# Windowed attention and FFN on one core: K and V blocks written from PSUM by two engines in place of DMA moves

## The chip, the cores and the metric

One Trainium2 chip, one core. The metric is the device time of one execution in microseconds (us), the median of the runs. Engines: PE is TensorE, DVE VectorE, ACT ScalarE, POOL GpSimd, SP SyncE (which here only issues DMAs).

## What is computed

Two layers of the same two blocks on x of 2048 rows by 512, in bf16: attention with 32 heads of 16 over a causal window of 256 keys, then a ReLU FFN of width 1792, each behind a layer norm and added to x.

```python
def _A_ref(x, wqkv, wo):
    H = 32; Dh = D // H; W = 256
    q, k, v = ...
    scores = jnp.einsum("bhqd,bhkd->bhqk", q, k) * (Dh ** -0.5)
    mask = (idx[:, None] - idx[None, :] >= 0) & (idx[:, None] - idx[None, :] < W)
    p = _softmax(jnp.where(mask[None, None], scores, -1e9), axis=-1)
    o = jnp.einsum("bhqk,bhkd->bhqd", p, v)
    return o.transpose(0, 2, 1, 3).reshape(B, S, D) @ wo
...
for layer in range(2):
    x = x + _A_ref(_layernorm(x), A_wqkv, A_wo)
    x = x + jnp.maximum(_layernorm(x) @ w1, 0) @ w2
```

## The kernel before

**Steps and slots.** The 2048 rows are cut into four chunks of 512 rows; two layers make eight steps, k = 0 to 7 (layer and chunk of a step are `divmod(k, 4)`). A step has twenty slots (`SPS`): four Q tiles t of 128 columns (eight heads of 16), and for each five groups g of key blocks (`GROUPS`, line 21). All 160 slots are written out in the loop at line 538. In a slot, in this order: the score matmuls of its group into the one score buffer `Sps` (`attn_group`, line 271, which ends with the exp on ScalarE into `Pb`); events planned for the slot; the first half of the slot's quota of projection and FFN matmuls (`run_tasks`); the masks of the group before (on VectorE, for groups 1 and 2 on GpSimd); the PV matmuls of the Q tile before, for one block of 128 rows (`pv_group`, into an accumulator `acc`, then VectorE's reciprocal and product into `O`); for the last Q tile of a step the DMA transpose of that row block of O into `OT` (`transpose_o`, line 344), whose output projection is planned two slots later; then the rest of the quota. So the PV matmuls of a step's last Q tile, its four OT transposes and its output projections O0 to O3 fall into slots 1 to 6 of the next step.

**Tasks.** A task is a group of 512-column matmuls into one PSUM bank of the pool `ps_d` (four banks, shared with `acc`) and its evacuation. The planner (`Task`, `run_tasks`, lines 403 to 432) takes among the tasks whose earliest slot has come the one with the earliest due time, and finishes it before it starts another. The quota of a slot is the number of matmuls left over the slots left, nine in most of the run and eight from step 6 on. `plan_qkv(k + 1)` plans the next chunk's K, Q and V for step k (lines 455 to 474). `plan_ffn` plans the FFN of a step when its fourth output projection is done; its w1 and w2 tasks run about one step later. `wo_done` (line 497) is called when an output projection's last matmul is issued: after O1 and after O3 it does half of the second norm (`ln_rows`: statistics on VectorE, power and products on GpSimd, then two DMA transposes into `xn2T` on SyncE's queue).

**Order.** Each engine's instructions go in the order in which the code issues them (`InOrder`, line 84), and SyncE's DMAs in one queue. An instruction that waits holds up all behind it on its engine.

**K.** K is needed as `KBD`: for each 64-key block two copies side by side, one with the odd heads' rows set to zero, one with the even heads' (e = 0, 1; the 16-row bands of a partition group). `KBD` is a ring of 20 blocks. In step 0 (`direct`) VectorE multiplies the PSUM bank by a 0/1 column of `par` per e, writing whole partitions. In the other steps ScalarE copies the bank to `Kst` (two buffers), and SyncE moves the bands, four per e, into `KBD`, whose other bands stay zero from the start (`k_items`, lines 220 to 246). Where a chunk's eight blocks wrap round the ring (the chunks made in steps 1 and 6) there are two runs of blocks, so 16 moves per tile and not 8.

**V.** `V2` holds per 64-key block two halves of 64 partitions, e = 0 and 1, 16 heads of 16 columns and a column of ones each. In step 0 VectorE copies four pieces of 64 partitions by 256 straight from PSUM; in the others it copies the bank to `Vst` (two buffers), and SyncE moves four pieces (`v_items`, lines 248 to 268).

**The chunk's norm.** `begin` (line 527) does the first norm of the next chunk in four slots from `SPS * k - 4`: statistics in slots 16 and 18 of the step before, application and the transposes into the one `xnT` buffer in slots 17 and 19. The Q tiles have five buffers.

Of the kernel before, what the change touches and what calls it, by code (L numbers as in the profile page):

```python
# [49 lines left out]
def kernel(  # L50
# [105 lines left out]
    KBD = const.tile([P, 4, NSLOT, 2, 64], BF16, name="KBD")  # L156
    V2f = const.tile([P, NSLOT * 544], BF16, name="V2f")
    V2 = V2f[:].rearrange("p (s e a d) -> p s e a d", s=NSLOT, e=2, a=16)
    Vst = [const.tile([P, 2, 16, 17], BF16, name=f"Vst{i}") for i in range(2)]
    for s0 in range(0, NSLOT, 4):  # L160
        nc.gpsimd.memset(V2f[:, 544 * s0:544 * (s0 + 4)].bitcast(FP32), 0.0)
        for e in range(2):
            nc.vector.memset(V2[64 * e:64 * e + 64, s0:s0 + 4, e, :, 16:17], 1.0)
    for t in range(4):
        nc.vector.memset(KBD[:, t, 8:NSLOT].rearrange("p a b c -> p (a b c)").bitcast(FP32), 0.0)
    for i in range(2):
        nc.vector.memset(Vst[i][:, :, :, 16:17], 1.0)
    PWALL = 20 * PW
    Pb = [const.tile([P, PWALL + 64], BF16, name=f"Pb{i}") for i in range(2)]
    for i in range(2):  # L170
# [38 lines left out]
    def q_items(xnT, Qt, t, direct=False):  # L209
        ps = []  # L210

        def one(kc):
            if kc == 0:
                ps.append(ps_d.tile([P, 512], FP32, name="ps_d"))
            mm(ps[0][:], wqkv[:, kc, t * P:(t + 1) * P], xnT[:, kc, :], kc == 0, kc == KC - 1)
            if kc == KC - 1:
                (act.copy if chained[0] and not direct else dve.tensor_copy)(Qt[:], ps[0][:])
        return [lambda kc=kc: one(kc) for kc in range(KC)]

    def k_items(layer, c, xnT, t, direct):  # L220
        ps = []
        s0 = slot(layer, 8 * c)
        runs = [(0, 8)] if s0 + 8 <= NSLOT else [(0, NSLOT - s0), (NSLOT - s0, 8)]

        def one(kc):
            if kc == 0:
                ps.append(ps_d.tile([P, 512], FP32, name="ps_d"))
            mm(ps[0][:], wqkv[:, kc, D + t * P:D + (t + 1) * P], xnT[:, kc, :], kc == 0, kc == KC - 1)
            if kc < KC - 1:
                return  # L230
            if not direct:
                Kst = work.tile([P, 512], BF16, name="Kst", bufs=2)
                act.copy(Kst[:], ps[0][:])
            for a, b in runs:
                sa = (s0 + a) % NSLOT
                for e in range(2):
                    if direct:
                        dve.tensor_scalar(out=KBD[:, t, sa:sa + b - a, e, :],
                                          in0=ps[0][:, 64 * a:64 * b].rearrange("p (s k) -> p s k", k=64),
                                          scalar1=par[:, e:e + 1], scalar2=None, op0=ALU.mult)  # L240
                        continue
                    for r in range(4):
                        rows = slice(32 * r + 16 * e, 32 * r + 16 * e + 16)
                        nc.sync.dma_start(KBD[rows, t, sa:sa + b - a, e, :],  # L244
                                          Kst[rows, 64 * a:64 * b].rearrange("p (s k) -> p s k", k=64))
        return [lambda kc=kc: one(kc) for kc in range(KC)]

    def v_items(layer, c, xnT, j, direct):
        ps = []

        def one(kc):
            if kc == 0:
                ps.append(ps_d.tile([P, 512], FP32, name="ps_d"))
            mm(ps[0][:], xnT[:, kc, j * P:(j + 1) * P], wqkv[:, kc, 2 * D:3 * D], kc == 0, kc == KC - 1)
            if kc < KC - 1:
                return
            v4 = ps[0][:].rearrange("p (a e d) -> p e a d", e=2, d=16)
            if not direct:
                dve.tensor_copy(Vst[j % 2][:, :, :, 0:16], v4)
            for half in range(2):  # L260
                sl = slot(layer, 8 * c + 2 * j + half)
                for e in range(2):
                    if direct:
                        dve.tensor_copy(V2[64 * e:64 * e + 64, sl, e, :, 0:16], v4[64 * half:64 * half + 64, e])
                    else:
                        nc.sync.dma_start(V2[64 * e:64 * e + 64, sl, e].rearrange("p a d -> p (a d)"),  # L266
                                          Vst[j % 2][64 * half:64 * half + 64, e].rearrange("p a d -> p (a d)"))
        return [lambda kc=kc: one(kc) for kc in range(KC)]


# [104 lines left out]
    def w2_items(c, hT, j, final):  # L375
        ps = []
        b = 4 * c + j

        def one(f):
            if f == 0:  # L380
                ps.append(ps_d.tile([P, 512], FP32, name="ps_d"))
            mm(ps[0][:], hT[:, f, j * P:(j + 1) * P], w2[:, f, :], f == 0, f == NF - 1)
            if f < NF - 1:
                return
            if final:
                ob = work.tile([P, D], BF16, name="ob", tag="Kst", bufs=2)
                dve.tensor_tensor(out=ob[:], in0=ps[0][:], in1=x_sb[:, b, :], op=ALU.add)
                nc.sync.dma_start(out_v[:, b, :], ob[:])
            else:
                dve.tensor_tensor(out=x_sb[:, b, :], in0=ps[0][:], in1=x_sb[:, b, :], op=ALU.add)  # L390
        return [lambda f=f: one(f) for f in range(NF)]
# [3 lines left out]
    SPS = 20  # L395
# [4 lines left out]
    def at_slot(s, fn):  # L400
        events.setdefault(s, []).append(fn)
# [53 lines left out]
    def plan_qkv(k, base):  # L455

        layer, c = divmod(k, NCH)

        def q_make(t):
            Q[k, t] = work.tile([P, 512], BF16, name="Qt", bufs=5)  # L460
            return q_items(xnTs[k], Q[k, t], t, k == 0)
        order = [("K0", 1), ("K1", 2.5), ("K2", 4), ("K3", 5.5), ("Q0", 7), ("V0", 8), ("V1", 9), ("V2", 10), ("V3", 11),
                 ("Q1", 12.5), ("Q2", 14.5), ("Q3", 17)]
        if k == 0:
            order = [("K0", 0), ("Q0", 0), ("V0", 1), ("V1", 1), ("V2", 1), ("V3", 1), ("K1", 2), ("Q1", 2), ("K2", 5),
                     ("Q2", 5), ("K3", 8), ("Q3", 8)]
        for what, due in order:
            n = int(what[1])
            if what[0] == "K":
                Task(base, base + due, base + SPS + 5 * n - 3, KC, lambda n=n: k_items(layer, c, xnTs[k], n, k == 0))  # L470
            elif what[0] == "Q":
                Task(base + 5 * n + 1 if k else 0, base + due, base + SPS + 5 * n - 1, KC, lambda n=n: q_make(n))
            else:
                Task(base + 7 if k else 0, base + due, base + SPS + 3, KC, lambda n=n: v_items(layer, c, xnTs[k], n, k == 0))

    def plan_ffn(k, s):
        layer, c = divmod(k, NCH)
# [48 lines left out]
    for k in range(NSTEP - 1):  # L526
        def begin(k=k, j=0, box={}):
            if j == 0:
                xnTs[k + 1] = work.tile([P, KC, 512], BF16, name="xnT", tag="xnT", bufs=1)
            if j % 2 == 0:  # L530
                box["s"] = ln_stats((k + 1) % NCH, "A", j, j + 2)
            else:
                ln_apply((k + 1) % NCH, xnTs[k + 1], "A", j - 1, j + 1, box["s"])
        for j in range(4):
            at_slot(max(2 + j // 2, SPS * k - 4 + j), lambda k=k, j=j, fn=begin: fn(k, j))
        plan_qkv(k + 1, SPS * k)
    masks = []
    for s in range(NS + 5):
# [88 lines left out]
    def run(items):  # L627
        for x in items:
            x()

    with tc.If(flag > 0):
# [64 lines left out]
```

## Time and profile before

| | us |
|---|---|
| median of 2 runs | 776.92 (776.37 to 777.47) |
| the profiled execution | 774.82 |
| its span, first to last instruction | 773.1 |
| PE busy | 527.7 (68%) |
| DVE busy | 330.2 (43%) |
| ACT busy | 317.1 (41%) |
| POOL busy | 254.2 (33%) |

The busy times are those of the profiled execution. Nearly all instructions have one line (94, the helper that records them), so groups are told apart by their tiles. SPq is SyncE's queue, whose instructions are DMA issues. PEclk is the granted TensorE clock as a share of 2.4 GHz; 0.50 is its lower level, 1.2 GHz. A window's row gives its limits and length, the busy us (and instructions) of PE, PEld, DVE, ACT and POOL, then PEclk, the DMA share and GB/s. A step's limits in time are the starts of its first exp and that of the next step's.

### The profile page before, as it was taken

How to read it: one execution, taken by the hardware profiler on the slowest of the kernel's cores; microseconds unless marked ns; L12 is line 12 of the kernel's file. 1: busy time of each engine (PE TensorE's matmuls, PEld its weight loads, DVE VectorE, ACT ScalarE, POOL GpSimd, SP SyncE). 2: the span in 40 equal slices, each digit the busy share in tenths (PEclk: the TensorE clock that was granted, in tenths of full speed). 3: DMA queues.
4: the chain of work that ended last, by engine and by line, in shares of the span. 5: the costliest groups of instructions: out<-in, count | busy, mean ns of one | idle time of the engine just before them, and what ended most of it. 6: DMA issues, size and time to landing. Idle time of an engine off the chain costs nothing.

```text
span 773.1 us, 14419 instructions
## 1 busy us (share of the span) xinstructions
PE 527.7 (68%) x5741; PEld 242.7 (31%) x5741; DVE 330.2 (43%) x869; ACT 317.1 (41%) x223; POOL 254.2 (33%) x558
## 2 busy tenths in 40 slices
PE   6656530459857797479857795579814689789576
PEld 2212310124323353134323342234301234434232
DVE  5822500237605472147515571257401455645541
ACT  2315722235544374345434353346513447736000
POOL 6432611042521345052523343053610342453100
PEclk8966565589968799778968898689966789979878
DMA  9312111121112211220212101220201210300200
GB/s 316 99 33 36 25 22 19 21 43 23 28 25 38 51 15 21 33 55 20 28 27 43 43 16 30 39 53 7 49 13 20 56 32 16 56 15 22 44 19 32
DMA packets 101244, 30.64 MB, mean 40 GB/s; under 512 B 85552, under 2 KB 100656, under 8 KB 101168
## 3 DMA queue, kind: packets, MB, share of 16 engines
q1 hardware_dynamic: 101168, 29.63, 17.9%
q8 instruction: 47, 0.77, 0.4%
q14 instruction: 29, 0.24, 0.1%
HBM read 7.86 MB, written 2.10 MB: 13 GB/s over the span
## 4 chain that ended last, share of the span: by engine, by line
PE 36%; SPq 22%; POOL 12%; DVE 11%; DMA 9%; issue 6%; ACT 3%; ACTq 0%; DVEq 0%; POOLq 0%
PE ps_d L94 28%; SPq L244 18%; PE acc L94 5%; POOL Pb L94 4%; PE Sps L94 4%; DMA OT<-O 4%; POOL xnA L94 3%; SPq L266 2%; DMA xnT<-xnA 2%; POOL xnB L94 2%; ACT Pb L94 2%; DVE stB L94 2%; DMA V2f<-Vst 2%; SPq L199 2%; DVE x_sb L94 1%
## 5 line engine op out<-in xcount | busy, mean ns | idle before, releaser
L94 ACT ACTIVATE Pb<-Sps 128x2048 bf16<-128x2048 f32 (+2 forms) x160 | 283.5, 1772 | 271.5 <-PE Sps L94 248.2
L94 POOL TENSOR_SCALAR_AFFINE_SELECT Pb<-Pb 64x256 bf16<-64x256 bf16 x368 | 154.4, 420 | 207.9 <-ACT Pb L94 182.9
L94 PE MATMUL ps_d<-xn2T,w 128*128 128x512 bf16 x448 | 128.7, 423 | 39.4 <-DMA xn2T<-xnB 25.4
L94 PE MATMUL ps_d<-wo,OT 128*128 128x512 bf16 x128 | 49.8, 541 | 102.6 <-DMA OT<-O 102.2
L94 PE MATMUL ps_d<-w,hT 128*128 128x512 bf16 x448 | 118.7, 395 | 0.8 <-DVE x_sb L94 0.8
L94 PEld LDWEIGHTS <-Pb 128*128 128x128 bf16 x2880 | 94.8, 99 | 46.7 <-issue 21.1
L94 PE MATMUL ps_d<-xnT,wqkv 128*128 128x512 bf16 x256 | 81.5, 445 | 37.4 <-DMA xnT<-xnA 33.1
L94 PE MATMUL acc<-V2f,Pb 128*128 128x34 bf16 x2880 | 96.3, 181 | 8.0 <-ACT Kst L94 4.5
L94 PE MATMUL Sps<-Qt,KBD 32*128 32x320 bf16 (+4 forms) x1408 | 67.6, 276 | 43.2 <-ACT Pb L94 42.1
L94 DVE TENSOR_TENSOR x_sb<-ps_d,x_sb 128x512 f32<-128x512 f32 x48 | 32.7, 689 | 148.1 <-PE ps_d L94 145.7
L94 DVE TENSOR_SCALAR hT<-ps_d 128x512 bf16<-128x512 f32 x112 | 76.8, 688 | 43.0 <-PE ps_d L94 42.6
L94 POOL TENSOR_TENSOR rstdB<-rstdB,mhalf 128x2 f32<-128x2 f32 x16 | 12.1, 759 | 200.8 <-DVE rstdB L94 200.8
L94 DVE RECIPROCAL chk<-acc 128x8 f32<-128x8 f32 x128 | 26.2, 204 | 117.7 <-PE acc L94 116.8
L94 PEld LDWEIGHTS <-w 128*128 128x128 bf16 x448 | 40.6, 104 | 93.6 <-issue 64.8
L94 DVE TENSOR_TENSOR Pb<-Pb,tri 128x512 bf16<-128x512 bf16 (+1 forms) x152 | 61.5, 436 | 16.1 <-ACT Pb L94 16.0
L94 PEld LDWEIGHTS <-KBD 32*128 32x128 bf16 x1408 | 24.7, 95 | 114.6 <-issue 112.0
L94 ACT CAST Kst<-ps_d 128x512 bf16<-128x512 f32 x28 | 16.0, 587 | 98.3 <-DMA KBD<-Kst 79.3
L94 PEld LDWEIGHTS <-OT 128*128 128x128 bf16 x128 | 13.1, 121 | 126.4 <-DMA OT<-O 109.1
L94 PEld LDWEIGHTS <-hT 128*128 128x128 bf16 x448 | 38.3, 100 | 44.8 <-issue 11.7
L94 DVE CAST Vst<-ps_d 128x512 bf16<-128x512 f32 x28 | 19.3, 690 | 67.0 <-DMA V2f<-Vst 53.8
L94 PEld LDWEIGHTS <-wqkv 128*128 128x128 bf16 x256 | 23.8, 107 | 71.3 <-issue 58.6
L94 DVE TENSOR_TENSOR O<-acc,chk 128x128 bf16<-128x128 f32 x128 | 37.3, 291 | 4.4
(66 smaller groups left out, 274.3 us busy)
## 6 DMA issues: line engine op xcount, KB each, us to landing
V2f<-Vst SPq DMA_DIRECT2D x112, 34.0 KB, 1.9
w<-in_B_w_dram SPq DMA_DIRECT2D x2, 1792.0 KB, 13.7
KBD<-Kst SPq DMA_DIRECT2D x160, 16.0 KB, 1.9
KBD<-Kst SPq DMA_DIRECT2D x128, 8.0 KB, 1.8
out_dram<-ob SPq DMA_DIRECT2D x16, 128.0 KB, 1.7
wqkv<-in_A_wqkv_dram SPq DMA_DIRECT2D x3, 512.0 KB, 6.3
xst<-in_A_x_dram SPq DMA_DIRECT2D x3, 512.0 KB, 8.7
xst<-in_A_x_dram SPq DMA_DIRECT2D x2, 256.0 KB, 2.9
```

Of the source, the lines that this page charges most:

```text
L94: inst = fn(*a, **k)
L199: nc.sync.dma_start_transpose(out=xnT[:, :, j * P:(j + 1) * P], in_=xn[:].rearrange("p (kc d) -> p kc d", kc=KC))
L244: nc.sync.dma_start(KBD[rows, t, sa:sa + b - a, e, :], Kst[rows, 64 * a:64 * b].rearrange("p (s k) -> p s k", k=64))
L266: nc.sync.dma_start(V2[64 * e:64 * e + 64, sl, e].rearrange("p a d -> p (a d)"), Vst[j % 2][64 * half:64 * half + 64, e].rearrange("p a d ...
```

## The change

K and V go from the PSUM bank to `KBD` and `V2` without `Kst`, `Vst` and DMA moves, in every step: VectorE writes e = 0 and ScalarE e = 1. The Q tiles get seven buffers, the due times of K, Q and V are changed (Q beside K, Q3 from slot 6 on), and the chunk's norm begins at `SPS * k - 7`.

```diff
-    Vst = [const.tile([P, 2, 16, 17], BF16, name=f"Vst{i}") for i in range(2)]
...
-    def k_items(layer, c, xnT, t, direct):
+    def k_items(layer, c, xnT, t):
...
-            if not direct:
-                Kst = work.tile([P, 512], BF16, name="Kst", bufs=2)
-                act.copy(Kst[:], ps[0][:])
             for a, b in runs:
                 sa = (s0 + a) % NSLOT
                 for e in range(2):
-                    if direct:
-                        dve.tensor_scalar(out=KBD[:, t, sa:sa + b - a, e, :],
-                                          in0=ps[0][:, 64 * a:64 * b].rearrange("p (s k) -> p s k", k=64),
-                                          scalar1=par[:, e:e + 1], scalar2=None, op0=ALU.mult)
-                        continue
-                    for r in range(4):
-                        rows = slice(32 * r + 16 * e, 32 * r + 16 * e + 16)
-                        nc.sync.dma_start(KBD[rows, t, sa:sa + b - a, e, :],
-                                          Kst[rows, 64 * a:64 * b].rearrange("p (s k) -> p s k", k=64))
+                    o = KBD[:, t, sa:sa + b - a, e, :]
+                    i = ps[0][:, 64 * a:64 * b].rearrange("p (s k) -> p s k", k=64)
+                    if e:
+                        act.activation(o, i, ACT.Copy, scale=par[:, 1:2])
+                    else:
+                        dve.tensor_scalar(out=o, in0=i, scalar1=par[:, 0:1], scalar2=None, op0=ALU.mult)
...
             v4 = ps[0][:].rearrange("p (a e d) -> p e a d", e=2, d=16)
-            if not direct:
-                dve.tensor_copy(Vst[j % 2][:, :, :, 0:16], v4)
             for half in range(2):
                 sl = slot(layer, 8 * c + 2 * j + half)
                 for e in range(2):
-                    if direct:
-                        dve.tensor_copy(V2[64 * e:64 * e + 64, sl, e, :, 0:16], v4[64 * half:64 * half + 64, e])
-                    else:
-                        nc.sync.dma_start(V2[64 * e:64 * e + 64, sl, e].rearrange("p a d -> p (a d)"),
-                                          Vst[j % 2][64 * half:64 * half + 64, e].rearrange("p a d -> p (a d)"))
+                    (act.copy if e else dve.tensor_copy)(V2[64 * e:64 * e + 64, sl, e, :, 0:16],
+                                                         v4[64 * half:64 * half + 64, e])
...
-                ob = work.tile([P, D], BF16, name="ob", tag="Kst", bufs=2)
+                ob = work.tile([P, D], BF16, name="ob", bufs=2)
...
-            Q[k, t] = work.tile([P, 512], BF16, name="Qt", bufs=5)
+            Q[k, t] = work.tile([P, 512], BF16, name="Qt", bufs=7)
...
-        order = [("K0", 1), ("K1", 2.5), ("K2", 4), ("K3", 5.5), ("Q0", 7), ("V0", 8), ("V1", 9), ("V2", 10), ("V3", 11),
-                 ("Q1", 12.5), ("Q2", 14.5), ("Q3", 17)]
+        order = [("K0", 1), ("Q0", 2), ("K1", 3), ("Q1", 4), ("K2", 5), ("Q2", 6), ("K3", 7), ("V0", 8), ("V1", 9), ("V2", 10),
+                 ("V3", 11), ("Q3", 12)]
...
-                Task(base + 5 * n + 1 if k else 0, base + due, base + SPS + 5 * n - 1, KC, lambda n=n: q_make(n))
+                Task(base + (6 if n == 3 else 1) if k else 0, base + due, base + SPS + 5 * n - 1, KC, lambda n=n: q_make(n))
...
-            at_slot(max(2 + j // 2, SPS * k - 4 + j), lambda k=k, j=j, fn=begin: fn(k, j))
+            at_slot(max(2 + j // 2, SPS * k - 7 + j), lambda k=k, j=j, fn=begin: fn(k, j))
```

The branch for extreme sums behind the loop (line 631), which this data does not take, gets the same K and V code.

## Rows read from the trace of the kernel before

**Rows 1.** The page's chain of waits: shares of the span by engine, by line
```profile
PE 36%; SPq 22%; POOL 12%; DVE 11%; DMA 9%; issue 6%; ACT 3%; ACTq 0%; DVEq 0%; POOLq 0%
PE ps_d L94 28%; SPq L244 18%; PE acc L94 5%; POOL Pb L94 4%; PE Sps L94 4%; DMA OT<-O 4%; POOL xnA L94 3%; SPq L266 2%; DMA xnT<-xnA 2%; POOL xnB L94 2%; ACT Pb L94 2%; DVE stB L94 2%; DMA V2f<-Vst 2%; SPq L199 2%; DVE x_sb L94 1%
```
**Rows 2.** Waits of the whole run: total us, times, longest us
```profile
PE ps_d L94 <- DMA OT<-O: 102.2, 15, 18.2
ACT Kst L94 <- DMA KBD<-Kst: 79.3, 14, 9.7
DVE Vst L94 <- DMA V2f<-Vst: 53.8, 8, 13.0
PE ps_d L94 <- DMA xnT<-xnA: 33.1, 7, 9.7
```
**Rows 3.** Windows by step (0, 1, 2-5, 6, 7): length; busy us; PEclk; DMA
```profile
22.40:95.10 72.70, 43.17 (x436) 19.46 (x434) 33.79 (x89) 33.19 (x28) 28.10 (x62) 0.70 0.18 37
95.10:206.90 111.80, 59.80 (x708) 28.16 (x709) 37.41 (x100) 41.72 (x29) 31.21 (x68) 0.72 0.14 25
206.90:550.10 343.20, 256.59 (x2849) 116.24 (x2848) 155.71 (x409) 157.72 (x113) 120.58 (x265) 0.84 0.18 33
550.10:653.80 103.70, 62.30 (x742) 28.82 (x741) 34.34 (x92) 41.47 (x28) 27.07 (x61) 0.79 0.14 29
653.80:717.20 63.40, 55.66 (x730) 28.02 (x729) 34.20 (x91) 37.54 (x20) 25.55 (x58) 0.92 0.14 31
```
**Rows 4.** Timeline of SyncE in step 3: start us, us
```profile
302.90 11.32 SPq L244 DMA_DIRECT2D KBD<-Kst  x16
314.32 1.22 SPq L346 DMA_TRANSPOSE OT<-O  x1
...
342.94 10.15 SPq L266 DMA_DIRECT2D V2f<-Vst  x16
```
**Rows 5.** Windows: after O3 in step 1; quiet slots; step 0's slots 10 to 19
```profile
160.20:164.30 4.10, 4.10 (x36) 1.70 (x40) 2.14 (x5) 0.00 (x0) 0.00 (x0) 0.52 0.00 0
351.40:380.20 28.80, 28.80 (x375) 14.31 (x374) 21.24 (x55) 19.73 (x13) 13.80 (x32) 0.99 0.12 16
632.10:653.80 21.70, 21.55 (x313) 11.14 (x312) 11.69 (x31) 15.97 (x10) 9.10 (x23) 1.00 0.03 8
75.50:95.10 19.60, 12.15 (x213) 7.55 (x211) 12.22 (x40) 13.42 (x10) 11.26 (x26) 0.50 0.14 30
```
**Rows 6.** Groups by form: busy us, mean ns of one
```profile
L94 ACT ACTIVATE Pb<-Sps 128x2048 bf16<-128x2048 f32 x136 | 255.4, 1878 | 233.6 <-PE Sps L94 210.3 <-DVE O L94 11.3 <-issue 5.7
...
L94 DVE CAST Vst<-ps_d 128x512 bf16<-128x512 f32 x28 | 19.3, 690 | 67.0 <-DMA V2f<-Vst 53.8 <-PE acc L94 8.7 <-PE ps_d L94 4.5
...
L94 ACT CAST Kst<-ps_d 128x512 bf16<-128x512 f32 x28 | 16.0, 587 | 98.3 <-DMA KBD<-Kst 79.3 <-PE ps_d L94 18.9
...
L94 DVE CAST V2f<-ps_d 64x256 bf16<-64x256 f32 x16 | 6.8, 424 | 1.6 <-PE ps_d L94 1.4
...
L94 DVE TENSOR_SCALAR KBD<-ps_d,par 128x512 bf16<-128x512 f32 x8 | 5.6, 742 | 2.9 <-PE ps_d L94 2.8
...
L94 ACT ACTIVATE xnA<-xst,nbS,rstdS 128x512 bf16<-128x512 bf16 x4 | 3.0, 805 | 10.6 <-POOL nbS L94 10.6
```
**Rows 7.** Timeline of step 1's slots 4 to 9, from O1 on
```profile
148.26 1.89 PE L94 MATMUL ps_d<-wo,OT 128*128 128x512 bf16 x4 [9.24 <-DMA OT<-O]
...
150.19 0.69 DVE L94 TENSOR_TENSOR x_sb<-ps_d,x_sb 128x512 f32<-128x512 f32 x1 [11.14 <-PE ps_d L94]
...
155.07 2.50 SPq L199 DMA_TRANSPOSE xn2T<-xnB  x2
157.68 1.21 SPq L346 DMA_TRANSPOSE OT<-O  x1
160.16 1.89 PE L94 MATMUL ps_d<-wo,OT 128*128 128x512 bf16 x4 [6.17 <-DMA OT<-O]
...
171.26 1.02 PE L94 MATMUL ps_d<-xn2T,w 128*128 128x512 bf16 x4 [1.05 <-issue]
```

More of the change, by code (lines that the diff above doesn't have):

```diff
@@ L165 @@
         nc.vector.memset(KBD[:, t, 8:NSLOT].rearrange("p a b c -> p (a b c)").bitcast(FP32), 0.0)
-    for i in range(2):
-        nc.vector.memset(Vst[i][:, :, :, 16:17], 1.0)
     PWALL = 20 * PW
@@ L236, in one, with v_items @@
                 for e in range(2):
-                    if direct:
-                        dve.tensor_scalar(out=KBD[:, t, sa:sa + b - a, e, :],
-                                          in0=ps[0][:, 64 * a:64 * b].rearrange("p (s k) -> p s k", k=64),
-                                          scalar1=par[:, e:e + 1], scalar2=None, op0=ALU.mult)
-                        continue
-                    for r in range(4):
-                        rows = slice(32 * r + 16 * e, 32 * r + 16 * e + 16)
-                        nc.sync.dma_start(KBD[rows, t, sa:sa + b - a, e, :],
-                                          Kst[rows, 64 * a:64 * b].rearrange("p (s k) -> p s k", k=64))
+                    o = KBD[:, t, sa:sa + b - a, e, :]
[4 more added lines that the diff above has]
+                        dve.tensor_scalar(out=o, in0=i, scalar1=par[:, 0:1], scalar2=None, op0=ALU.mult)
         return [lambda kc=kc: one(kc) for kc in range(KC)]
-    def v_items(layer, c, xnT, j, direct):
+    def v_items(layer, c, xnT, j):
         ps = []
@@ L469, in plan_qkv @@
             if what[0] == "K":
-                Task(base, base + due, base + SPS + 5 * n - 3, KC, lambda n=n: k_items(layer, c, xnTs[k], n, k == 0))
+                Task(base, base + due, base + SPS + 5 * n - 3, KC, lambda n=n: k_items(layer, c, xnTs[k], n))
             elif what[0] == "Q":
-                Task(base + 5 * n + 1 if k else 0, base + due, base + SPS + 5 * n - 1, KC, lambda n=n: q_make(n))
+                Task(base + (6 if n == 3 else 1) if k else 0, base + due, base + SPS + 5 * n - 1, KC, lambda n=n: q_make(n))
             else:
-                Task(base + 7 if k else 0, base + due, base + SPS + 3, KC, lambda n=n: v_items(layer, c, xnTs[k], n, k == 0))
+                Task(base + 7 if k else 0, base + due, base + SPS + 3, KC, lambda n=n: v_items(layer, c, xnTs[k], n))
     def plan_ffn(k, s):
@@ L650 @@
                 for t in range(4):
-                    Qts.append(work.tile([P, 512], BF16, name="Qt", bufs=5))
-                    run(q_items(xnT, Qts[t], t) + k_items(layer, c, xnT, t, True))
+                    Qts.append(work.tile([P, 512], BF16, name="Qt", bufs=7))
+                    run(q_items(xnT, Qts[t], t) + k_items(layer, c, xnT, t))
                 for j in range(4):
-                    run(v_items(layer, c, xnT, j, True))
+                    run(v_items(layer, c, xnT, j))
                 O = work.tile([P, 4, D], BF16, name="O", tag="O", bufs=1)
```

## The prediction

> **What bounds the kernel now.** I read the chain of waits first, since no engine is busy for more than 68% of the span. Its shares by engine and by line [rows 1] give 22% to SyncE's queue, and name two lines: 18% of the chain is the issuing of the K moves (line 244), 2% that of the V moves (line 266). The reader is to see that an engine which computes nothing stands on the path. The list of waits [rows 2] says who pays: ScalarE stood 79.3 us before its K copies until an earlier K move had landed (there are two Kst buffers), VectorE 53.8 us before its V copies, TensorE 102.2 us until a transposed O had landed and 33.1 us for the next chunk's normalised rows. SyncE's own instructions [rows 4] tie these together: sixteen K moves take 11.32 us, some 0.7 us each, an OT transpose comes between two such batches, and sixteen V moves take 10.15 us. So the OT that TensorE waits for stands behind K moves in one queue.
>
> What would be left without this? I cut the span at the first exp of each step, twenty slots to a step [rows 3]: steps 2 to 5 take 343.2 us together (85.8 each), step 1 111.8 and step 6 103.7; in these two the next chunk's K wraps round the ring and needs 16 moves per tile in place of 8. Step 7, which makes no K or V, takes 63.4. Slots 10 to 19 of step 3 take 28.80 us with TensorE busy throughout [rows 5], so 2.88 us for a slot of nine projection or FFN matmuls; with eight it is 2.73 (21.70 for eight slots of step 6 [rows 5]). A step of such slots would take 57.6.
>
> **The change part by part.**
>
> 1. *The moves go.* 288 K and 112 V issues leave SyncE, and the waits for them with it: Kst and Vst no longer exist. What is taken back is the difference between the steps of now and steps of quiet slots, less what is late next. The next parts work that out.
>
> 2. *K written by two engines.* Per K tile ScalarE's copy of 587 ns goes, VectorE gets a multiply of 742 ns (as in step 0 now) and ScalarE one activation with a per-partition scale, which lies between that copy and the 805 ns of the activation with scale and bias [rows 6]; I take 0.7. ScalarE needs 1.88 us of a slot for its exp [rows 6] and so has a microsecond free; VectorE has 21.24 of 28.80 us busy in the quiet stretch [rows 5], and less where no FFN is evacuated. What is not hidden is that ScalarE's half, if the two engines take turns on the bank, delays the next exp where a tile ends late in a slot. Bounds: 0, if the exp's slack covers all, and 4 tiles times 0.74, so 3.0 a step. I take 1.2, nearer the lower, because only two of the four tiles end in the second half of a slot. In steps 1 and 6 each tile is cut in two: 2.0.
>
> 3. *V written by two engines.* Per V tile one VectorE copy goes and four pieces of 64x256 come, two on each engine. VectorE's cost 424 ns [rows 6]. ScalarE's are not in the trace; from its exp of 2048 elements and its copy of 512, 1.878 and 0.587 [rows 6], follow 0.84 ns an element and 0.16 us fixed, so 0.38 us for 256. Slots 7 and 8 of a step hold two V tiles each, eight pieces. If the engines read side by side, ScalarE needs 1.88 + 4 x 0.38 = 3.40 us, 0.52 over a quiet slot; that is the lower end. If they take turns, V0's first VectorE piece hides behind the exp, and after it follow 0.38, 0.42, 0.38, then V1's 0.42, 0.38, 0.42, 0.38: 2.78, with hand-overs some 3.3, so a slot of 5.2. The next exp stands behind these pieces on ScalarE, and the next score matmuls wait for the exp, since there is one score buffer. I take 5.2, so 2 x 2.3 = 4.6 a step: nowhere in this trace do two engines read one accumulator, every copy there comes out of it on one engine after the matmuls, and in the code each piece of ScalarE follows one of VectorE in the same bank.
> The Trainium skill, "PSUM — Partial Sum Buffer", section "PSUM bank collisions raise a hardware error", says that two engines on one bank and quadrant at once collide, reads against reads included, so that software has to put them in turn. No run here shows it yet. By that rule the slot is the 5.2 taken here; without it, the first rival below.
>
> 4. *The norm three slots sooner, Q3 and Q2 sooner, seven Q tiles.* The xnT transposes now come in slots 14 and 16 in place of 17 and 19, and TensorE first needs them in slot 1 of the next step, where it came to them in slot 0. There is one xnT buffer, so this needs every reader of the old one to be done; with the new due times Q3 is issued in slot 6 and V3 in slot 8, long before. The 33.1 us wait [rows 2] goes, and no DMA stands behind these transposes in SyncE's queue but the next OT, five slots later. The two added Q buffers let Q0 to Q2 of the next chunk be written in slots 2 to 5 while this step's four are still read; no wait comes of them. The norm's statistics now meet the FFN's evacuations on VectorE in slots 13 and 15, some 3.7 us of work in slots of 2.88; the four accumulators hold most of that. 0.5 a step, bounds 0 and 1.6 (twice the overshoot).
>
> 5. *What is late next: the fourth OT.* Following the planner's rule through the new due times, the previous FFN's last task ends in slot 1 (before: slot 4), and the output projections O0 to O3 fall into slots 3, 4, 5 and 6, where before O1 came in slot 5. O1's end calls the first half of the second norm, so its two transposes are put on SyncE's queue in the first half of slot 4, ahead of the OT of the fourth row block, which is put there in the second half. They wait for O1, the statistics, and GpSimd. In the trace of before step 1 happens to have this order [rows 7]: O1 starts at 148.26, the add at 150.19, the two transposes leave at 155.07, the OT at 157.68, and O3 starts at 160.16 after an idle of 6.17 us. From the add to O3 is 9.97 us; with O1's four matmuls at full clock, 0.9 in place of 1.9, O3 comes 11.1 us after O1's start. The planned distance is two slots, 5.8 us: 5.3 us late. After it the clock is low: 4.10 us at 0.52 for eight matmuls and one PV [rows 5], where a whole slot with eight takes 2.73; 1.6 for the restart. So 6.9 a step. Bounds: 0, and with none of the planned distance 11.1 + 1.6 = 12.7. In step 1 slots 3 to 5 are short (five, four, four matmuls), which takes 0.8 off and makes O3 0.8 later; in step 6 O3 comes a slot later and 4.4 remains.
> The FFN's first matmul comes 11.1 us after O3 (160.16 to 171.26 [rows 7]); between them lie the rest of slot 6, 2.5, and two slots of 5.2, so no wait there.
>
> 6. *Step 0* loses its moves too. Bounds: 0 and 72.7 - 57.6 = 15.1; most of the excess is the first chunk's norm, which stays, so 6. Step 7 and the tail hold none of the change: 0.
>
> **The sum.** A step of 2 to 5: 57.6 + 1.2 + 4.6 + 0.5 + 6.9 = 70.8, four of them 283.2 against 343.2: 60.0 saved. Step 1: 57.6 + 2.0 + 4.6 + 0.5 + 6.9 = 71.6 against 111.8: 40.2. Step 6: 20 x 2.73 + 2.0 + 4.6 + 4.4 = 65.6 against 103.7: 38.1. With step 0, 144.3. The profiled execution took 774.82 with a span of 773.1; 774.82 - 144.3 = 630.5. The median of the runs, 776.92, is 2.1 above it: 633.
>
> **The rivals.**
>
> *Both engines read side by side.* Slots 7 and 8 then cost 0.52 more and not 2.3: 3.6 less a step, 21 in six: 612. For it: the pieces write different partitions and only read the same bank. Against it: nothing of the kind in the trace. Chance 0.2.
>
> *The fourth OT is not late,* because VectorE and GpSimd, with nothing else to do in slot 4, finish the second norm's first half sooner, or the plan is slower than 2.88 there. 6.9, five times, and 4.4 go: 594. Against it [rows 7], where VectorE and GpSimd were free as well. Chance 0.12.
>
> *The clock stays at its lower level through slots 0 to 9.* With O3's idle and slots that wait for ScalarE, TensorE might not get back to 2.4 GHz. Slots 10 to 19 of step 0, busy 12.15 of 19.60 us, ran at 0.50 throughout [rows 5]. A low slot costs at least 4.10 - 2.73 = 1.4 more, about 2 with its scores; seven slots beyond those priced, 13 a step, 79 in all: 712. Against it: steps 2 to 5 now, with longer idles in just these slots, stand at 0.84 as a whole [rows 3]. Chance 0.15.
>
> *Slower than before:* the same mechanism through all of steps 1 to 6, the quiet halves too, since exps held back by ScalarE's new pieces would thin out TensorE's work. 2 us a slot on 120 slots is 240: about 873. It decides from 72 slots on (144 / 2). For it the row at 0.50; against it 0.99 in the quiet stretch [rows 5] and 0.92 over step 7 [rows 3], whose slots change little. Chance 0.03.
>
> **How the numbers follow.** Forecast 0.45, rivals 0.2, 0.12, 0.15, 0.03; 0.05 for the first two together (573 before the FFN's first matmul is late again, some 584). All but the last lie more than 2% (about what a measurement of this kernel can tell from no change) under 776.9, and partial forms of the slow one, 68 to 76 low slots, would be within it: faster 0.95, same 0.02, slower 0.03. The range goes from 594, the second rival, to 690, which takes in K at its upper bound (11 in six steps) and half of the third rival; the rest of that one and the case of 584 are left out.
>
> **What would show it.** No DMA from Kst or Vst; SyncE's queue nearly gone from the chain; VectorE about 349 us busy (330.2 + 28 x 0.742 + 56 x 0.424 - 19.3 for Vst [rows 6], less half of the K and V pieces that it writes for step 0 now) and ScalarE about 347; slots 10 to 19 of a step at 29 us as now. Part 3 is right if ScalarE's V pieces in a slot alternate with VectorE's and the exps there are 5.2 apart; if the pieces overlap, the first rival holds. Part 5 is right if in steps 1 to 5 TensorE idles some 5 us before O3, released by an OT that left SyncE right behind two xn2T transposes. It would be wrong if the largest idle of a step stands elsewhere, or if a step takes more than 80 us.

## The result and the profile after

The changed kernel took 620.38 us, median of 2 runs (618.08 to 622.68), against 776.92 before: a ratio of 0.7985, 95% interval 0.7855 to 0.8115. The forecast of 633 lay 2% above it. The twelfth experiment below times the same kernel again on another chip: 620.89 us, 0.8001 (0.7964 to 0.8037). The profiled execution took 618.08 with a span of 616.4, against 774.82 and 773.1.

The page's chain of waits of the changed kernel, by engine and by line, to be set against [rows 1].

```profile
PE 53%; ACT 16%; DVE 14%; DMA 5%; POOL 5%; issue 3%; SPq 2%; POOLq 0%; ACTq 0%; DVEq 0%
PE ps_d L94 40%; ACT Pb L94 12%; PE acc L94 7%; PE Sps L94 6%; DMA OT<-O 4%; DVE V2f L94 3%; ACT V2f L94 3%; DVE stB L94 2%; SPq L196 2%; POOL xnB L94 2%; DVE x_sb L94 2%; DVE KBD L94 2%; POOL rstdB L94 1%; DVE O L94 1%; DMA xnT<-xnA 1%
```

SyncE's queue has fallen from 22% of the chain to 2%, and more than half of the chain is now TensorE's own work. What is left of DMAs on the path is mainly the OT, 4%, as before.

The waits of the whole run (total us, times, longest), to be set against [rows 2]:

```profile
PE ps_d L94 <- DMA OT<-O: 39.1, 14, 6.3
ACT KBD L94 <- DVE KBD L94: 37.9, 25, 8.4
...
DVE V2f L94 <- ACT V2f L94: 32.9, 32, 2.3
ACT V2f L94 <- DVE V2f L94: 30.7, 48, 7.2
...
PE ps_d L94 <- DMA xnT<-xnA: 6.7, 1, 6.7
```

The two waits for K and V moves are gone, and that for xnT has one instance left, in step 0. New are three lines in which ScalarE and VectorE wait for each other. They are waits of an engine, not yet losses; which of them the path feels is what the experiments are for.

The windows by step (0, 1, 2 to 5, 6), cut as in [rows 3]:

```profile
22.30:87.20 64.90, 38.74 (x437) 18.46 (x438) 31.41 (x84) 40.85 (x48) 29.28 (x63) 0.75 0.13 32
87.20:158.40 71.20, 58.63 (x716) 28.19 (x715) 41.95 (x113) 45.53 (x40) 31.66 (x68) 0.89 0.12 23
158.40:429.30 270.90, 232.64 (x2847) 113.09 (x2847) 168.28 (x440) 170.28 (x145) 121.09 (x264) 0.94 0.14 26
429.30:499.50 70.20, 58.32 (x737) 28.22 (x736) 39.15 (x104) 45.51 (x41) 25.61 (x58) 0.93 0.13 22
```

Of the 156.7 us that left the span, step 0 gave 7.8, step 1 40.6, steps 2 to 5 72.3, step 6 33.5, and step 7, the head and the tail 2.5. The matmuls are the same; TensorE's busy time fell all the same, from 527.7 to 492.1 us, as the granted clock rose in each of these windows. Of the 35.6 us, 24.0 lie in steps 2 to 5, where it went from 0.84 to 0.94.

The timeline of step 3 around the output projections (start us, us, engine, operation, idle before and its releaser), which answers to [rows 7]:

```profile
238.70 1.03 PE L94 MATMUL ps_d<-wo,OT 128*128 128x512 bf16 x4
243.08 0.29 DVE L94 TENSOR_TENSOR O<-acc,chk 128x128 bf16<-128x128 f32 x1
...
244.64 2.50 SPq L196 DMA_TRANSPOSE xn2T<-xnB  x2
...
245.89 0.74 DVE L94 TENSOR_SCALAR KBD<-ps_d,par 128x512 bf16<-128x512 f32 x1
246.66 0.69 ACT L94 ACTIVATE KBD<-ps_d,par 128x512 bf16<-128x512 f32 x1 [3.06 <-DVE KBD L94]
247.25 1.87 ACT L94 ACTIVATE Pb<-Sps 128x2048 bf16<-128x2048 f32 x1
247.31 1.19 SPq L332 DMA_TRANSPOSE OT<-O  x1
249.77 1.89 PE L94 MATMUL ps_d<-wo,OT 128*128 128x512 bf16 x4 [5.34 <-DMA OT<-O]
```

The first row is O1, the last O3. The fourth block of O was written at 243.37, but its OT left SyncE at 247.31, right behind the two xn2T transposes that O1's norm had put in front of it. O3 starts 11.07 us after O1 and 5.34 us late; its four matmuls take 1.89 us where O1's took 1.03. In the middle stands something that I had not priced in this form: ScalarE's half of K3 waits 3.06 us for VectorE's half, which is queued there behind statistics, masks and checks, and the exp stands behind it.

The windows of slots 10 to 19 of step 3 and of the stretch after O3, against [rows 5]:

```profile
266.40:295.00 28.60, 28.60 (x375) 14.36 (x374) 20.25 (x51) 18.78 (x11) 15.81 (x34) 1.00 0.10 20
...
249.80:253.60 3.80, 3.80 (x36) 1.72 (x40) 1.87 (x4) 0.00 (x0) 0.00 (x0) 0.58 0.00 0
```

A quiet slot takes 2.86 us, against 2.88 before. After O3 the granted clock was 0.58 over 3.80 us.

The V pieces on VectorE and ScalarE in slot 7 of step 3, up to the exp of slot 8:

```profile
254.14 1.88 ACT L94 ACTIVATE Pb<-Sps 128x2048 bf16<-128x2048 f32 x1
...
256.05 0.37 ACT L94 CAST V2f<-ps_d 64x256 bf16<-64x256 f32 x1
256.45 0.43 DVE L94 CAST V2f<-ps_d 64x256 bf16<-64x256 f32 x1 [1.07 <-ACT V2f L94]
...
256.91 0.37 ACT L94 CAST V2f<-ps_d 64x256 bf16<-64x256 f32 x1 [0.49 <-DVE V2f L94]
...
257.36 0.41 DVE L94 CAST V2f<-ps_d 64x256 bf16<-64x256 f32 x1
...
257.80 0.37 ACT L94 CAST V2f<-ps_d 64x256 bf16<-64x256 f32 x1 [0.52 <-DVE V2f L94]
...
259.05 1.88 ACT L94 ACTIVATE Pb<-Sps 128x2048 bf16<-128x2048 f32 x1
```

The pieces of one tile alternate, and each of these begins 0.03 to 0.08 us after the other engine's has ended. VectorE's at 256.45 reads partitions 64 to 127 of the bank and ScalarE's at 256.05 reads 0 to 63, and still one waits for the other: the turns are taken over the whole accumulator. The exps are 4.91 us apart.

### The profile page after: what moved, and what is told of

It reads as the page before. It is cut to its first block, busy times and chain, and to the rows that moved or that the text cites. A ratio compares the mean times of both kernels' runs of the same rounds, so it can differ in the third digit from the quotient of the medians.

```text
span 616.4 us, 13901 instructions
## 1 busy us (share of the span) xinstructions
PE 492.1 (80%) x5741; PEld 237.4 (39%) x5741; DVE 348.9 (57%) x919; ACT 345.9 (56%) x299; POOL 255.0 (41%) x558
## 4 chain that ended last, share of the span: by engine, by line
PE 53%; ACT 16%; DVE 14%; DMA 5%; POOL 5%; issue 3%; SPq 2%; POOLq 0%; ACTq 0%; DVEq 0%
PE ps_d L94 40%; ACT Pb L94 12%; PE acc L94 7%; PE Sps L94 6%; DMA OT<-O 4%; DVE V2f L94 3%; ACT V2f L94 3%; DVE stB L94 2%; SPq L196 2%; POOL xnB L94 2%; DVE x_sb L94 2%; DVE KBD L94 2%; POOL rstdB L94 1%; DVE O L94 1%; DMA xnT<-xnA 1%
## 5 line engine op out<-in xcount | busy, mean ns | idle before, releaser
L94 PE MATMUL ps_d<-xn2T,w 128*128 128x512 bf16 x448 | 118.9, 400 | 14.7 <-DMA xn2T<-xnB 13.2
L94 PE MATMUL ps_d<-w,hT 128*128 128x512 bf16 x448 | 110.8, 381 | 0.0
L94 PEld LDWEIGHTS <-Pb 128*128 128x128 bf16 x2880 | 92.6, 97 | 34.9 <-issue 9.1
L94 PE MATMUL Sps<-Qt,KBD 32*128 32x320 bf16 (+4 forms) x1408 | 64.6, 266 | 48.2 <-ACT Pb L94 46.8
L94 PE MATMUL ps_d<-xnT,wqkv 128*128 128x512 bf16 x256 | 78.1, 423 | 8.3 <-DMA xnT<-xnA 6.7
L94 PE MATMUL ps_d<-wo,OT 128*128 128x512 bf16 x128 | 40.3, 443 | 39.1 <-DMA OT<-O 39.1
L94 DVE CAST V2f<-ps_d 64x256 bf16<-64x256 f32 x64 | 27.0, 421 | 35.7 <-ACT V2f L94 32.9
L94 ACT ACTIVATE KBD<-ps_d,par 128x512 bf16<-128x512 f32 (+1 forms) x40 | 24.1, 604 | 38.2 <-DVE KBD L94 37.9
L94 DVE TENSOR_SCALAR KBD<-ps_d,par 128x512 bf16<-128x512 f32 (+1 forms) x40 | 25.5, 639 | 31.6 <-PE ps_d L94 21.1
L94 ACT CAST V2f<-ps_d 64x256 bf16<-64x256 f32 x64 | 23.5, 368 | 31.2 <-DVE V2f L94 30.7
```

Of the source, the lines that this page charges most:

```text
L94: inst = fn(*a, **k)
```

## The experiments

Each ratio is to the kernel before, run on the same chip. "Slot lengths" are distances between the starts of successive exps.

**1. The direct writes alone.** Order, Q buffers and norm as before the change.

```diff
-Q[k, t] = work.tile([P, 512], BF16, name="Qt", bufs=7)
+Q[k, t] = work.tile([P, 512], BF16, name="Qt", bufs=5)
...
+order = [("K0", 1), ("K1", 2.5), ("K2", 4), ("K3", 5.5), ("Q0", 7), ("V0", 8), ("V1", 9), ("V2", 10), ("V3", 11),
+         ("Q1", 12.5), ("Q2", 14.5), ("Q3", 17)]
...
+Task(base + 5 * n + 1 if k else 0, base + due, base + SPS + 5 * n - 1, KC, lambda n=n: q_make(n))
...
-at_slot(max(2 + j // 2, SPS * k - 7 + j), lambda k=k, j=j, fn=begin: fn(k, j))
+at_slot(max(2 + j // 2, SPS * k - 4 + j), lambda k=k, j=j, fn=begin: fn(k, j))
```

> The changed kernel with the old due times, five Q tiles and the old place of the norm: K and V written by the two engines, nothing else. Theory: the moves were the bound, and the new order brings no more than it costs. A step of 2 to 5 then has 57.6 us of quiet slots, 3.7 us of wait for the normalised rows in slot 0 with about 1 of restart, V's 4.1, K's 0.5, and no late fourth OT, since the second norm's first half is called in slot 5, behind it: some 67 us, so 610 to 628 us in all. Rival: the sooner norm and Q tiles are needed as well; then the waits for xnT and OT stay above 60 us together and the time is over 640.

Measured: 622.18 us, ratio 0.8033 (0.7986 to 0.808), within the theory's range and the same as the whole change. Its waits and TensorE's first projection matmul in step 3:

```profile
PE ps_d L94 <- DMA xnT<-xnA: 29.9, 7, 6.8
...
PE ps_d L94 <- DMA OT<-O: 10.4, 6, 6.6
```
```profile
239.54 1.01 PE L94 MATMUL ps_d<-xnT,wqkv 128*128 128x512 bf16 x2 [3.66 <-DMA xnT<-xnA]
```

The xnT wait of before stays, some 3.6 us in each of steps 2 to 6, and the OT's is 10.4 in place of 39.1. So the writes alone bring all that the change brings. The order, the buffers and the norm take away one wait (29.9 us to 6.7) and make another of about that size (10.4 to 39.1).

**2. The second norm out of the fourth OT's way.** The first half of the norm is called after O2, when the last OT has been issued, and the second after O3.

```diff
-        if j % 2:
-            ln_rows(c, xn2T[k], "B", j - 1, j + 1)
+        if j >= 2:
+            ln_rows(c, xn2T[k], "B", 2 * j - 4, 2 * j - 2)
```

> The changed kernel with the first half of the second norm called at the end of O2 (slot 5) in place of O1 (slot 4), so that the fourth OT stands ahead of its two transposes in SyncE's queue. Theory: the idle of 5.3 us before O3 and the 1.6 of restart go in steps 1 to 6, O3 comes at the start of slot 6, and the FFN's first matmul, 11 us after O3, still finds its rows because slots 7 and 8 take 4.9 each: 575 to 588 us. Rival: the wait only moves to the FFN's first matmul (its rows come as late as before, 13 us or more after slot 6 begins), and less than 15 us are won: over 605.

Measured: 594.37 us, 0.7687 (0.7642 to 0.7733), between the theory and the rival. Step 3, O3 and then K3:

```profile
235.74 1.04 PE L94 MATMUL ps_d<-wo,OT 128*128 128x512 bf16 x4
...
238.52 0.69 ACT L94 ACTIVATE KBD<-ps_d,par 128x512 bf16<-128x512 f32 x1 [3.57 <-DVE KBD L94]
...
239.10 1.87 ACT L94 ACTIVATE Pb<-Sps 128x2048 bf16<-128x2048 f32 x1
```

O3 waits no more in steps 2 to 5 (over the whole run TensorE's waits for an OT fall from 39.1 to 5.6 us), and slot 6 falls from 6.9 us to 2.45. But slot 5 stays at 5.2 to 6.2: ScalarE's half of K3 still waits for VectorE's. Under O3's wait that cost nothing, as the ninth experiment shows; without it, it is paid, some 3 us a step.

**3. V by engine, not by half.** VectorE's two pieces of a tile, then ScalarE's two.

```diff
-            for half in range(2):
-                sl = slot(layer, 8 * c + 2 * j + half)
-                for e in range(2):
+            for e in range(2):
+                for half in range(2):
+                    sl = slot(layer, 8 * c + 2 * j + half)
```

> The changed kernel with the two loops over a V tile's pieces exchanged: VectorE's two pieces come first, then ScalarE's two; the pieces, their engines and their times are the same. Theory: the 4.9 us of slots 7 and 8 are hand-overs between two engines that take turns on one bank; with one hand-over per tile ScalarE has 1.88 + 4 x 0.37 = 3.4 us and the slots take 3.3 to 3.7: 600 to 608 us. Rival: it is ScalarE's or VectorE's own queue that fills these slots, whatever the order: they stay within 0.3 us of 4.9 and the time within 5 us of 620.

Measured: 599.73 us, 0.7745 (0.7701 to 0.7788), 0.3 us below the theory's range. Slot 8 falls from 4.91 to 3.45 us, slot 7 to 4.4. Step 3, the exps of slots 8 and 9:

```profile
252.08 1.88 ACT L94 ACTIVATE Pb<-Sps 128x2048 bf16<-128x2048 f32 x1
...
255.52 1.88 ACT L94 ACTIVATE Pb<-Sps 128x2048 bf16<-128x2048 f32 x1
```

**4. Both, the second and the third.**

> Both edits together: norm half after O2, and V's pieces two and two. Theory: both gains, 41 and 17, less a wait of about 1 us a step at the FFN's first matmul, since slots 7 and 8 no longer cover the 11 us from O3: 563 to 577 us. Rival: the second norm's chain from O3 (11 us against three slots of some 9.5) takes back V's gain whole: 580 or more.

Measured: 578.54 us, 0.7468 (0.7424 to 0.7512), in the gap between the two. The gains nearly add up: 0.0314 and 0.0256 below the 0.8001 of the changed kernel, and 0.0533 together. Slot 5's 5.2 to 6.3 us stay. The granted clock from step 2 to step 4 is 0.99.

**5. ScalarE first on K.** One word of the changed kernel.

```diff
-                for e in range(2):
+                for e in (1, 0):
```

> The changed kernel with ScalarE's half of each K tile written ahead of VectorE's; all else as changed. Theory (what the second experiment laid bare was hidden before by the fourth OT): slot 5 of a step falls from 5.5 us to some 3.2, because ScalarE's K3 half, and the exp behind it, no longer wait for VectorE's queue; but O3 is still bound by the fourth OT, and slot 6 grows by about as much, from 6.9 to some 9. Time 612 to 620, so within a per cent of the changed kernel's 620. Rival (the 2.5 us of slot 5 are a cost of their own, beside O3's wait): they go, 6 times 2.5, and the time is 605 or less.

Measured: 626.13 us, 0.8101 (0.8067 to 0.8135): 1% slower than the changed kernel, which neither had said. Slot 5 falls to some 3 us, as both said, and slot 6 grows from 6.9 to 11.4 and more. Step 3, from O1 to O3:

```profile
242.65 1.03 PE L94 MATMUL ps_d<-wo,OT 128*128 128x512 bf16 x4
...
245.08 0.75 DVE L94 TENSOR_SCALAR KBD<-ps_d,par 128x512 bf16<-128x512 f32 x1 [3.01 <-ACT KBD L94]
...
255.73 1.89 PE L94 MATMUL ps_d<-wo,OT 128*128 128x512 bf16 x4 [7.30 <-DMA OT<-O]
```

Now VectorE is the one that waits: its half of K2 stands 3.01 us for ScalarE's, which stands behind an exp, and O1's add and the norm stand behind it. O3 comes 13.08 us after O1 in place of 11.07. So the theory's mechanism held (slot 5's cost was hidden), and the edit moved the wait to the engine whose queue leads to O3.

**6. ScalarE first on K and V, with the norm of the second.** The edits of the second and the fifth, and V as in the third with `for e in (1, 0)`.

> The second norm's halves after O2 and O3, and ScalarE's pieces ahead of VectorE's in both K and V, so that the next exp never stands behind a wait for VectorE. Theory: against the fourth experiment (578.5), a step loses the 3 us that slot 5 still has over a quiet slot, 0.7 in slot 1 and about 1.2 in slot 7; of these some 1.5 come back as a wait of the FFN's first matmul for the transposes of the second norm, since fewer microseconds lie between O3 and it: 3 to 4 us in each of six steps, 554 to 566. Rival (VectorE's own lateness is the limit, so what ScalarE no longer waits for, score banks or accumulators do): 572 or more.

Measured: 582.64 us, 0.7549 (0.7504 to 0.7594): the rival held, and it is no better than the fourth. In step 3, VectorE's K2, O3, and the FFN's first matmul:

```profile
222.59 0.75 DVE L94 TENSOR_SCALAR KBD<-ps_d,par 128x512 bf16<-128x512 f32 x1 [3.01 <-ACT KBD L94]
...
227.58 1.04 PE L94 MATMUL ps_d<-wo,OT 128*128 128x512 bf16 x4 [2.02 <-DMA OT<-O]
...
239.22 1.65 PE L94 MATMUL ps_d<-xn2T,w 128*128 128x512 bf16 x6 [2.83 <-DVE V2f L94]
```

What ScalarE no longer waits for, VectorE does: at K2 before the products into O, so that O3's OT is late again, and at V3, whose accumulator the FFN needs.

**7. K on VectorE alone,** else as the sixth.

```diff
-                    if e:
-                        act.activation(o, i, ACT.Copy, scale=par[:, 1:2])
-                    else:
-                        dve.tensor_scalar(out=o, in0=i, scalar1=par[:, 0:1], scalar2=None, op0=ALU.mult)
+                    dve.tensor_scalar(out=o, in0=i, scalar1=par[:, e:e + 1], scalar2=None, op0=ALU.mult)
```

> As the run before, but both halves of each K tile on VectorE, none on ScalarE, V with ScalarE's pieces first. Theory: K needs no second engine; what counts is that ScalarE's exp doesn't wait for VectorE. VectorE has four times 0.74 us more in a step in slots where it has room, so about the same time as the run before, 555 to 568. Rival (splitting K is worth its 0.7 us a tile, as it delays the second norm's statistics in slots 5 and 6 on VectorE): no gain over the fourth experiment, 576 or more.

Measured: 569.61 us, 0.7374 (0.7335 to 0.7414); 1.6 us above the theory's range, and 13 below the sixth, from which only K's second engine is gone. The sixth waited 50.3 us in VectorE's K multiplies for ScalarE. Of the 11.3 us between the two profiled spans, 8.5 lie in steps 1 and 6, whose K tiles are written in four pieces, 3.5 in steps 2 to 5 and 2.1 in step 7, head and tail; step 0 is 2.9 longer. Here O3 comes with 0.38 us of idle, and what is late is the FFN's first matmul, by 2.94:

```profile
224.00 1.04 PE L94 MATMUL ps_d<-wo,OT 128*128 128x512 bf16 x4 [0.38 <-DMA OT<-O]
...
236.40 1.45 PE L94 MATMUL ps_d<-xn2T,w 128*128 128x512 bf16 x6 [2.94 <-DMA xn2T<-xnB]
```

**8. The chunk's norm late again,** order and Q buffers as changed.

```diff
-        at_slot(max(2 + j // 2, SPS * k - 7 + j), lambda k=k, j=j, fn=begin: fn(k, j))
+        at_slot(max(2 + j // 2, SPS * k - 4 + j), lambda k=k, j=j, fn=begin: fn(k, j))
```

> The changed kernel with the chunk's norm back in slots 16 to 19 of the step before; the new order and the seven Q tiles stay. Theory (the earlier norm takes away what is left of the wait for the chunk's transposed rows, the new due times only bring the first use of them to slot 1): the wait comes back, now in slot 1, with 1 to 2 us a step: 625 to 632. Rival A (with the first projection matmul brought to slot 1 the earlier norm isn't needed): 618 to 622 as the changed kernel. Rival B (the wait is as large as in the first experiment, 4 us a step and a restart at low clock): 645 or more.

Measured: 637.39 us, 0.8239 (0.8199 to 0.8279), between the theory and rival B. Slot 1 of steps 2 to 5 grows by 1.0 to 1.6 us, as the theory said. Steps 1 and 6 lose 5.8 and 4.9, with the wait in slot 0. The first row is of step 1, the second of step 2:

```profile
94.78 3.83 PE L94 MATMUL ps_d<-xnT,wqkv 128*128 128x512 bf16 x9 [5.24 <-DMA xnT<-xnA]
171.25 0.59 PE L94 MATMUL ps_d<-xnT,wqkv 128*128 128x512 bf16 x2 [1.28 <-DMA xnT<-xnA]
```

With the first experiment this takes the small parts asunder. The new order (with its Q buffers) costs 0.021 of the time of before, 0.8239 against 0.8033, some 16 us: TensorE's waits for an OT are 38.9 us in place of the first's 10.4, those for xnT 19.6 in place of 29.9. In that order, the norm three slots sooner gives back 0.024, some 18.

**9. K on VectorE alone, nothing else.** The edit of the seventh on the changed kernel.

> The changed kernel with both halves of each K tile on VectorE and none on ScalarE; all else as changed. Theory (while O3 waits for the fourth OT, a K tile costs only what it adds between O1 and the second norm's statistics): slots 1 and 5 lose their excess, but O1's add comes 0.74 us later behind VectorE's second half, so O3 starts some 11.8 us after O1 in place of 11.1, slot 6 grows to about 10, and the time is 617 to 623. In the fifth experiment it was 13.1 after O1, because VectorE's half waited 3.0 us for ScalarE's. Rival (slot 5's 2.5 us or the taking of turns cost time by themselves): 608 or less.

Measured: 613.02 us, 0.7898 (0.785 to 0.7946), between the two. O1 and O3 of step 3:

```profile
235.49 1.03 PE L94 MATMUL ps_d<-wo,OT 128*128 128x512 bf16 x4 [0.16 <-issue]
...
247.41 1.49 PE L94 MATMUL ps_d<-wo,OT 128*128 128x512 bf16 x3 [6.05 <-DMA OT<-O]
```

11.92 us, where the theory said 11.8; slot 6 is 10.0. Steps 2 to 5 take 271.7 us, against the 270.9 of the changed kernel (274.3 in the trace of the twelfth experiment): there the split of K is no clear gain or loss. The 1% that is left is not in these steps. Steps 0, 1 and 6 are 1.4, 1.8 and 2.4 shorter, the last two being those whose K tiles are written in four pieces; why step 0 is shorter stays open.

**10. The second norm 3 and 1,** on the seventh.

```diff
-            ln_rows(c, xn2T[k], "B", 2 * j - 4, 2 * j - 2)
+            ln_rows(c, xn2T[k], "B", 3 * j - 6, j + 1)
```

> The seventh experiment with the second norm cut 3 and 1: the first three row blocks after O2, the last one after O3. Theory (there the FFN's first matmul waits some 3 us for the last transposes of xn2T): the chain behind O3 loses one block's statistics, 0.84, one application, 0.76, and one transpose, 1.25, so most of that wait in slot 9 goes, 2 to 3 us in five steps: 554 to 562. Rival (GpSimd or SyncE's queue still works on the three blocks when O3 is done, so the last block comes no sooner): 566 or more.

Measured: 566.52 us, 0.7298 (0.7252 to 0.7343), the shortest of all, but within the intervals of the seventh. The rival's time, by a third way: the transposes come sooner, and the FFN's first matmul waits for its accumulator instead, until VectorE's last V pieces end.

```profile
234.42 0.85 DVE L94 CAST V2f<-ps_d 64x256 bf16<-64x256 f32 x2
235.34 1.46 PE L94 MATMUL ps_d<-xn2T,w 128*128 128x512 bf16 x5 [2.50 <-DVE V2f L94]
```

**11. VectorE first on V again,** on the tenth.

> The tenth experiment with VectorE's two pieces of each V tile ahead of ScalarE's. Theory (there the FFN's first matmul waits 2.5 us not for the second norm but for the accumulator that VectorE's last V pieces hold, since they stand behind PV work on VectorE): VectorE's pieces end earlier, slot 9 falls from 3.2 to 4.6 us to some 3, slot 7 grows by about 1 as in the fourth experiment, so 1 us less a step at the most: 558 to 566. Rival (with VectorE first, the exp waits for VectorE again, and slot 7 gives more than slot 9 takes): 568 or more.

Measured: 568.68 us, 0.7343 (0.7312 to 0.7374): inside the rival's range, and not to be told from the tenth by the intervals. What slot 9 gains, slot 7 loses: the one falls to 2.43 us, and the other rises to between 6.1 and 6.7 in steps 2 to 5, since the exp waits for VectorE again.

**12. The changed kernel again.**

> The changed kernel once more, unaltered, in five rounds on the chip of the run before, for a narrower interval than its first two times give. Both theories: 617 to 624, a ratio of 0.795 to 0.806; so that the first (all but the direct writes undone), fifth (ScalarE first on K) and ninth (K on VectorE alone) experiments can be set against it by their ratios.

Measured: 620.89 us, 0.8001 (0.7964 to 0.8037), as both said. Against it the ninth (0.785 to 0.7946) is faster, the fifth (0.8067 to 0.8135) and the eighth slower, and the first the same. Its trace shows how far one execution of a kernel differs from another: in steps 3, 4 and 5 slot 10 ran at a granted clock of 0.58 to 0.62 and took 3.8 to 4.1 us, where in the first trace only step 5 has this.

```profile
399.62:403.67 4.05, 4.05 (x18) 1.26 (x17) 2.05 (x4) 1.88 (x2) 0.00 (x0) 0.58 0.00 0
```

The row is slot 10 of step 5 in the first trace; in step 3 there, slot 10 takes 2.46 us.

Not tried: the new order with the DMA moves kept, since the two added Q tiles need the room of Vst; and two engines reading one bank at the same time, since the semaphores of the program put them in turn.

## Why the prediction was right, point by point

*1, the moves.* Right: no packet of Kst or Vst is left, and the chain shows it. The first experiment shows that this part alone makes the whole gain.

*2, K.* Direction right, place wrong. I priced 1.2 a step as an exp delayed late in a slot. The cost in slot 5 was 2.5 (5.35 on the mean of steps 2 to 5), but O3's wait, which I had priced separately, covered it; the ninth experiment, which takes the split away, leaves steps 2 to 5 where they were. In the split steps 2.0 was about right (1.8 and 2.4 there). Laid bare, in the second experiment, it costs 3 us, the upper bound: not by the 0.7 us of a piece, but because each engine waits for the other's queue.

*3, V.* Right. The pieces take turns and the exps are 4.91 us apart, priced 5.2; VectorE's piece took 0.42 and ScalarE's 0.37, estimated at 0.38. Over quiet slots of 2.86 that is 4.1 a step, priced 4.6. The prediction set this beside the rule of the Trainium skill ("PSUM — Partial Sum Buffer", section "PSUM bank collisions raise a hardware error") that two engines must not be on one bank and quadrant at once, where a quadrant is 32 partitions. The trace, at 4.91, agrees with pieces in turn, but it is no test of that rule: the turns come from the program's semaphores, and no run let the engines read one bank together. Nor does the rule by itself ask for 5.2, as the prediction has it, since VectorE's second piece waits for a ScalarE piece on other partitions; what a slot takes with turns by quadrant, no run shows. That the order and not the reading is the price, the third experiment shows: with two turns a tile in place of four the slot takes 3.45, which is near the first rival's 3.40.

*4, the norm.* The wait goes but for the 6.7 us in step 0, and the eighth experiment shows its size: without the earlier norm some 18 us more. The 0.5 a step for VectorE did not come: slots 13 and 15 of step 3 took 2.99 and 2.46, as good as the 2.92 and 2.46 of the first experiment, which has the norm elsewhere.

*5, the fourth OT.* Right, in place, cause and size: 11.07 us from O1 to O3 (11.1), 5.34 of idle (5.3), a restart at 0.58 of the clock. That it fits to 0.03 us is in part luck. The terms given there come to 10.9 and not 11.1 (the row's 11.9 with 0.9 for O1's matmuls in place of 1.9), and these matmuls took 1.03. The second experiment shows the cause by moving the transposes away: the wait goes, and the time falls by 3.1% of that before. That is some 24 us, of the 39 that the part priced; slot 5's K cost, bare from then on, takes 11 of the rest in steps 2 to 5.

*6, step 0.* 7.8 where I had 6.

*The sum.* Steps 2 to 5 came to 67.7 each in place of 70.8. Slots 4 to 6 hold 6.9 over quiet ones, which is O3's price alone, so K's 1.2 is covered; 0.6 on the mean is V, 0.5 the norm's price, and the rest the other slots, of which the last ten took 2.85 on the mean. Step 1 came to 71.2 (71.6) with errors of both signs: its slots 0 and 1 took 3.7 over quiet ones, where K was priced 2.0, since besides the split K tiles the first nine projection matmuls took 4.02 us at a granted clock of 0.50, as step 0 left it. Step 6 is the term that was too small, 70.2 in place of 65.6. Its slots 0 to 2 lost 2.8 to the split K tiles, priced 2.0. O2 waited too, 1.21 us for its own OT, with a restart behind it (four matmuls in 1.89 us, at a granted clock of 0.50), so that slot 4 took 5.49 in place of 2.73. And slot 7, where O3's wait and the first two V tiles meet, took 10.29, since VectorE's product into O, which has one buffer, waited for the same OT:

```profile
444.31 1.89 PE L94 MATMUL ps_d<-wo,OT 128*128 128x512 bf16 x4 [1.21 <-DMA OT<-O]
...
457.41 1.53 PE L94 MATMUL ps_d<-wo,OT 128*128 128x512 bf16 x4 [4.15 <-DMA OT<-O]
457.49 0.29 DVE L94 TENSOR_TENSOR O<-acc,chk 128x128 bf16<-128x128 f32 x1 [4.54 <-DMA OT<-O]
```

In all 12 us more went than the 144 that were forecast: 12.3 more in steps 2 to 5, 1.8 in step 0, 0.4 in step 1 and 2.5 in step 7, head and tail, less 4.6 in step 6. The busy times said in advance, 349 for VectorE and 347 for ScalarE, came to 348.9 and 345.9. Of the rivals, the first fell with the alternating pieces and the second with O3's idle. The two of the clock fell as they were priced, with 0.94 in steps 2 to 5; but the low clock does come back in a slot 10 here and there, some 1.5 us each time, as the twelfth experiment has it.

## What to carry to other kernels

When a queue of moves is taken off the path, look through the plan for what is issued to that queue next, in what order; here that gave the largest wait that was left, with its cause and its size. Two engines that empty one accumulator in turns are coupled: each of them waits in the other's queue, and the wait lands on whichever path leaves the second one. So one engine with time to spare did better for K than two that took turns: by 13 us where O3's wait was gone, most of it in the two steps with K tiles in four pieces, and by 1% where it was not. A wait that is covered is not free: it is paid as soon as its cover is taken away, as slot 5 was.

## What the runs showed of the hardware that I had not expected

ScalarE copied 64x256 from PSUM faster than VectorE, 0.368 us on the mean against 0.421, and applied a scale to 128x512 in 0.687 against VectorE's 0.744 (the forms of the changed kernel, whose last columns are total us, mean ns, and the idle before):

```profile
L94 DVE CAST V2f<-ps_d 64x256 bf16<-64x256 f32 x64 | 27.0, 421 | 35.7 <-ACT V2f L94 32.9 <-PE ps_d L94 2.2
...
L94 ACT CAST V2f<-ps_d 64x256 bf16<-64x256 f32 x64 | 23.5, 368 | 31.2 <-DVE V2f L94 30.7
L94 DVE TENSOR_SCALAR KBD<-ps_d,par 128x512 bf16<-128x512 f32 x24 | 17.9, 744 | 14.3 <-PE ps_d L94 14.3
L94 ACT ACTIVATE KBD<-ps_d,par 128x512 bf16<-128x512 f32 x24 | 16.5, 687 | 32.3 <-DVE KBD L94 32.0
```

And turns go by accumulator, each of which has a bank of its own. In step 3 of the tenth experiment ScalarE wrote its four pieces of two V tiles without a break, 0.38 us each, and VectorE began on the first of the tiles as soon as ScalarE went on to the second; side by side on two banks, neither took more than 0.012 us longer than the means above.

```profile
232.29 1.52 ACT L94 CAST V2f<-ps_d 64x256 bf16<-64x256 f32 x4
...
233.07 0.86 DVE L94 CAST V2f<-ps_d 64x256 bf16<-64x256 f32 x2 [1.47 <-ACT V2f L94]
```
